# A K set between the first two Q sets, and two PSUM banks exchanged

## The chip, the cores and the metric

The kernel runs on one core of one Trainium2 chip. The metric is device time in microseconds. The engines are TensorE (PE in the profile, its weight loads apart as PEld), VectorE (DVE), ScalarE (ACT), GpSimd (POOL) and SyncE (SP), which issues most DMAs. Matrix products are written to PSUM, which this kernel divides into eight tiles of 128 x 512 fp32, called banks here.

## What is computed

Two branches read the same x (2048 rows of 512, bfloat16) and are mixed by a gate per row, g = sigmoid(sum(x * gate_w)):

- Branch B is an MLP: layer norm, product with w1 (512 x 1376), gelu, product with w2.
- Branch A is attention with a recurrent memory. The 2048 rows are cut into 64 segments of 32. Eight memory rows stand ahead of each segment, and attention runs over these 40 rows with 32 heads of 128:

```python
mem = mem0
for s in range(n_seg):                                  # 64, one after the other
    h = jnp.concatenate([mem, x[:, 32*s:32*s+32]], axis=1)      # 40 rows
    q, k, v = h @ Wq, h @ Wk, h @ Wv                    # 32 heads of 128
    p = softmax(where(mask, q @ k.T * scale, -1e9))
    o = (p @ v) @ Wo
    mem = o[:, :8]                                      # goes into the next segment
    outs.append(o[:, 8:])
out = g * concat(outs) + (1 - g) * mlp(x)
```

Segment s + 1 cannot project its memory rows before the attention of segment s has ended. The whole loop hangs on this recurrence.

## The kernel before

The program has three stages. First it does nearly all of the MLP (lines 299 to 598) while the attention weights are loaded; nine of its sixteen 128-row tiles are finished there, and for seven the second product is left over as filler. Then comes the loop over 64 segments (line 756), and last a short tail. The order of every instruction on every engine is written out by hand (a manual schedule); semaphores are added where one engine reads what another wrote, or overwrites what another still reads.

Four segments make a tile of 128 rows; T is the tile and si = 0..3 the segment's place in it. Of a segment's 40 rows, 32 are worked on in the loop itself: 24 rows of x and the 8 memory rows. They lie transposed in hT, which has four chunks (kc = 0..3) of 128 input features each. The other 8 rows of every segment, which are known ahead, are projected for a whole tile at once as filler work of the tile before.

One segment does, on TensorE in this order:

- Q and K of the 32 rows (lines 777 to 786). There are four groups: Q's first half of the heads, K's first half, Q's second half, K's second half. Group n is accumulated in bank U[n]. A group has four **sets**, one for each chunk kc of hT, and a set is four matmuls, one for each 32-column strip of the array (qk_unit, line 125). After each group ACT copies the bank to SBUF as bfloat16 (qk_cast, line 131) and DVE transposes the copy into QT or KT (qk_tr, line 136). After the first group DVE also writes the mask into U[0] (mask_put(1), line 257), where the second half of the scores is going to be.
- Scores of the first half (line 805), which read QT and KT, then the V sets in X1 and X2, sums of exponentials, scores of the second half.
- Attention times V (av, line 283), into all four U banks. ACT copies the result out: the memory's part into UT, the rest into XR.
- The output projection (wo_pass, line 736) into X2, which ACT copies to w in three pieces.
- The new memory (new_mem, line 744) in three calls, one for each piece of w. Call 0 makes chunk 0 of the next hT through bank U[0], call 1 chunk 1 through U[1], call 2 chunks 2 and 3 through a part of bank SbF. After each call DVE casts the product into hT (line 752). So the first Q set of the next segment needs the first cast, the second set the second, and the third and fourth sets the third.

Filler sets are spread between these steps by run(n). WS (line 755) says how many go where; one filler set goes between call 0 and call 1 and one between call 1 and call 2. A segment has eight filler sets. With si = 0 only five have gone by the first call, so that one set is left behind call 2; with other si none is left. In the last tile there is less filler.

In segments with si = 0, from the third tile on, extra (line 643) puts the finished rows of tile T - 2 together in a bank (out_sel, line 227) just before the first new_mem call. DVE reads that bank (line 238) after the third cast.

The lines that matter here, of the loop and of new_mem:

```python
for n, (t, hf) in enumerate(((0, 0), (1, 0), (0, 1), (1, 1))):
    bk = U[n]
    for kc in range(KC):
        qk_unit(bk, hc, t, hf, kc)
...
bk = (U[0][:, 0:M], U[1][:, 0:M], xs8z)[n]          # new_mem
```

Of the kernel before, what the change touches and what calls it, by code (L numbers as in the profile page):

```python
# [28 lines left out]
def kernel(ctx, tc, A_x, A_mem0, A_Wq, A_Wk, A_Wv, A_Wo, A_seg_len, B_x, B_w1, B_b1, B_w2, B_b2, gate_w, out):  # L29
# [4 lines left out]
    M = A_mem0.shape[1]  # L34
# [4 lines left out]
    KC = Dm // P  # L39
# [71 lines left out]
    U = [lps.tile([P, 512], FP32, name=f"U{i}") for i in range(4)]  # L111
# [13 lines left out]
    def qk_unit(bk, G, t, hf, kc):  # L125
        h0, h1 = HF[hf]
        for j in range(4):
            nc.tensor.matmul(bk[32 * j:32 * j + 32, :], lhsT=G[:, kc, :], rhs=W5[t][:, kc, h0:h1, j, :],  # L128
                             start=(kc == 0), stop=(kc == KC - 1), tile_position=(0, 32 * j))
# [57 lines left out]
    def vp_load(T, si):  # L187
        nc.sync.dma_start(VP[T % 2][:, si].rearrange("p v e -> p (v e)"), VLs[T][si:P:SPT].rearrange("p a v e -> p a (v e)"))
# [20 lines left out]
    def c_load(T):  # L209
        c = cw.tile([P, Dm], BF16, tag="c", name="c")  # L210
        nc.sync.dma_start(c[:], c_dr[T * P:(T + 1) * P, :])
        cs[T] = c
# [14 lines left out]
    def out_sel(T, bk):  # L227
        for si in range(SPT):
            nc.tensor.matmul(bk[32 * si:32 * si + 32, :], lhsT=SelR[:], rhs=ws.pop(SPT * T + si)[:], start=True, stop=False,
                             skip_group_check=True, tile_position=(0, 32 * si))  # L230
        wl = wls.pop(T)
        for si in range(SPT):
            nc.tensor.matmul(bk[32 * si:32 * si + 32, :], lhsT=SelL[:, 32 * si:32 * si + 32], rhs=wl[:], start=False, stop=True,
                             skip_group_check=True, tile_position=(0, 32 * si))

        def ev():
            o = cw.tile([P, Dm], BF16, tag="o", bufs=1, name="o")
            nc.vector.scalar_tensor_tensor(out=o[:], in0=bk[:], scalar=g_all[:, T:T + 1], in1=cs.pop(T)[:], op0=ALU.mult, op1=ALU.add)
            nc.sync.dma_start(out2[T * P:(T + 1) * P, :], o[:])
        dve_q.append(ev)  # L240
        yield

    def prep_h(s):
        T, si = divmod(s, SPT)
        nc.gpsimd.tensor_copy(out=hT[s % 3][:, :, 0:RIDE], in_=xTs[T][:, :, seg * si:seg * si + RIDE])
# [386 lines left out]
    def side(T, si):  # L632
        gens = []
        if si == 2:
            gens = [wo_left(T - 1, X1) if T >= 1 else mlp_units(8)]
        elif T + 1 == NT:
            gens = [mlp_units(4)] if si < 2 else []
        else:
            gens = [[left_qk(T + 1, 0, 0, X1), left_qk(T + 1, 1, 0, U[3])], [left_qk(T + 1, 0, 1, X1), left_qk(T + 1, 1, 1, U[3])], [],
                    [left_v(T + 1, 0, X1), left_v(T + 1, 1, U[3])]][si]  # L640
        return chain(*gens)

    def extra(T, si):

        if si == 0 and T >= 2:
            return out_sel(T - 2, U[2])
        return iter(())

    work = [(T, fc) for T in DEF for fc in range(FC)]
# [48 lines left out]
    xs8z = SbF[:, 4 * EW + NG:4 * EW + NG + 2 * M]  # L698
# [30 lines left out]
    def x_norm(s):  # L729
        T, si = divmod(s, SPT)  # L730
        XR, Rb = XRs.pop(s), Rbs.pop(s)[:].rearrange("p (c q) (h j) -> p h j c q", c=4, h=2)
        for out, o, a, b in ((UT[(s + 1) % 2], M, LEFT, 32), (UL[T % 2], LEFT * si, 0, LEFT)):
            for h in range(2):
                nc.gpsimd.tensor_tensor(out=out[:, :, 4 * h:4 * h + 4, o:o + b - a], in0=XR[:, :, 4 * h:4 * h + 4, a:b], in1=Rb[:, h, :, :, a:b], op=ALU.mult)  # L734
# [6 lines left out]
            nc.scalar.copy(out=w[:, a:b], in_=bk[:, a:b])  # L741
        return w

    def new_mem(w, hn, n):

        k0, nk = ((0, 1), (1, 1), (2, 2))[n]
        bk = (U[0][:, 0:M], U[1][:, 0:M], xs8z)[n]
        for k in range(nk):
            for c in range(4):
                nc.tensor.matmul(bk[32 * c:32 * c + 32, M * k:M * k + M], lhsT=w[:, (k0 + k) * P + 32 * c:(k0 + k) * P + 32 * c + 32], rhs=SelM[:],  # L750
                                 start=n < 2, stop=True, skip_group_check=True, tile_position=(0, 32 * c))
        nc.vector.tensor_copy(out=hn[:, k0:k0 + nk, RIDE:32], in_=bk.rearrange("p (k m) -> p k m", k=nk))  # L752


    WS = ((2, 2, 1), (2, 2, 2), (2, 2, 2), (2, 2, 2))
    for s in range(nseg):
        T, si = divmod(s, SPT)
        last = s == nseg - 1
        hc, hn = hT[s % 3], hT[(s + 1) % 3]
        W1, W2, W3 = WS[si]  # L760
        fill = side(T, si)
        if s + 1 < nseg:
            prep_h(s + 1)
        if s >= 1:
            x_norm(s - 1)
        if si == 0 and T >= 2:
            c_load(T - 2)
        if si < 3:
            vp_load(T, si + 1)
        if last:  # L770
            c_load(T - 1)
            c_load(T)
        if si == 0 and T + 2 < NT:
            load_xT(T + 2)
        if s in (2, (NT - 1) * SPT):
            hm_load4()
        for n, (t, hf) in enumerate(((0, 0), (1, 0), (0, 1), (1, 1))):
            bk = U[n]
            for kc in range(KC):
                qk_unit(bk, hc, t, hf, kc)  # L780
            if n == 0:
                flush(act_q, 9)
                flush(dve_q, 9)
            qk_tr(qk_cast(bk[:]), (QT, KT)[t], hf, LEFT * (1 - t))
            if n == 0:
                mask_put(1)
        V = cw.tile([P, NG, Dh], BF16, tag="V", name="V")
        E = cw.tile([P, NG, EW], BF16, tag="E", name="E")
        R = cw.tile([P, NG * 40], FP32, tag="R", name="R")
        Rs[s] = R  # L790
        xsum = SbF[:, 0:32 * NG].rearrange("p (i q) -> p i q", q=32)

        def exps(i2, x):
            c = slice(0, 40) if x else slice(40, EW)
            nc.scalar.activation(out=E[:, 4 * i2:4 * i2 + 4, c], in_=Sb[i2][:, :, c], func=ACTF.Exp, scale=scale)  # L795

        def msum(i2):
            sums(U[1 + 2 * i2][:, 320:352].rearrange("p (i q) -> p i q", q=8), E[:, 4 * i2:4 * i2 + 4, :], 40, 48, 8, True)

        def mnorm(i2):  # L800
            r, e = RP[i2], E[:, 4 * i2:4 * i2 + 4, 40:56].rearrange("p i (a q) -> p i a q", q=8)
            nc.vector.reciprocal(out=r, in_=U[1 + 2 * i2][:, 320:352])
            nc.vector.tensor_tensor(out=e, in0=e, in1=r.rearrange("p (i q) -> p i q", q=8).unsqueeze(2).to_broadcast([P, 4, 2, 8]), op=ALU.mult)

        scores(s, 0)
        nc.scalar.activation(out=E[:, 0:4, :], in_=Sb[0], func=ACTF.Exp, scale=scale)
        for kc in range(KC):
            v_unit(X1, hc, 0, kc)

        def v_cast(vb, h):  # L810
            i0 = 4 * vb + 2 * h
            nc.scalar.copy(out=V[:, i0:i0 + 2, :].rearrange("p i e -> p (i e)"), in_=(X1, X2)[vb][:, 256 * h:256 * h + 256])  # L812

        v_cast(0, 0)
        v_unit(X2, hc, 1, 0)
        if not last:
            xsums(E, 0)
            msum(0)
            mnorm(0)
        scores(s, 1)  # L820
        exps(1, 0)
        v_cast(0, 1)
        exps(1, 1)
        for kc in range(1, KC - 1):
            v_unit(X2, hc, 1, kc)
        if not last:
            if s:
                next(mlp, None)
            msum(1)
            mnorm(1)  # L830
        v_unit(X2, hc, 1, KC - 1)
        for h in range(2):
            v_cast(1, h)
        if last:
            break
        run(W1)
        if s:
            next(mlp, None)
        xsums(E, 1)
        recip_x(s)  # L840
        av(s, V, E)
        for j in (0, 2, 1, 3):
            nc.scalar.copy(out=UT[s % 2][:, j, :, 0:M], in_=U[j][:, 0:NG * 40].rearrange("p (i q) -> p i q", q=40)[:, :, 32:40])  # L843
        x_raw(s)
        run(W2)
        prep_q(s + 1)
        w = wo_pass(UT[s % 2], (0, P, 2 * P, Dm), X2)
        if s >= 1:
            ws[s - 1] = w
        run(W3)  # L850
        for _ in extra(T, si):
            pass
        new_mem(w, hn, 0)
        run(1)
        new_mem(w, hn, 1)
        run(1)
        new_mem(w, hn, 2)
        for _ in fill:
            pass
        if si == 3 and T + 2 < NT:  # L860
            left_x(T + 2)
        flush(dve_q, 9)
        nc.vector.tensor_tensor(out=rmin[:, 0:RW], in0=rmin[:, 0:RW], in1=R[:, 0:RW], op=ALU.min)
        flush(act_q, 9)
# [193 lines left out]
```

## Time and profile before

| | |
|---|---|
| median of 3 runs | 759.55 us (757.79 to 761.52) |
| profiled execution | 759.91 us, of which the span is 758.1 us |
| granted TensorE clock in it | 0.999 |
| TensorE busy | 741.6 us, 98% of the span |
| ACT, DVE, POOL busy | 71%, 53%, 36% |
| the loop over segments | from 80.4 us on; a segment takes about 10.2 to 10.5 us |

A row of the timeline gives the start in us from the start of the span, the duration, the engine, the line, the operation, output and inputs, shapes and the count of instructions that were merged into the row; in square brackets stands how long the engine was idle before it and what ended that. A row of the waits gives the engine and line that waited, what it waited for, the total in us, the number of times and the longest. Matmuls are pipelined: one of 512 columns has a duration of 0.38 us, but the next set starts long before it ends, so times between starts are what counts. The number before a bank or buffer is left out in the profile: U is any of U[0] to U[3].

### The profile page before, as it was taken

Reading aid. Unit: us, or ns where it says so; the run is one execution under the profiler, and the core shown is the slowest. Engines: PE = TensorE matmul, PEld = TensorE weight load, DVE = VectorE, ACT = ScalarE, POOL = GpSimd, SP = SyncE. Lnnn points to the kernel's source line nnn. Section 1 sums busy time; section 2 is a strip of 40 time slices with the busy share of each in tenths; the row PEclk is TensorE's granted clock in tenths of the full one; section 3 lists DMA queues with packets and bytes.
Section 4 is the critical chain, followed back from the end, with each engine's and each line's share of the span. In section 5 each row is a group of like instructions: output and inputs, shape, how many; then the busy total and the mean of one; then the engine's idle time right before and its main releaser. Section 6 shows DMA issues by size and latency. Waiting matters only on the chain.

```text
span 758.1 us, 45047 instructions
## 1 busy us (share of the span) xinstructions
PE 741.6 (98%) x19742; PEld 423.4 (56%) x19742; DVE 398.5 (53%) x1414; ACT 537.3 (71%) x1628; POOL 274.8 (36%) x517
## 2 busy tenths in 40 slices
PE   8999999999999999999999999999999999999997
PEld 5776455555555555555555556555555555555554
DVE  5767544545455545446454545445454545455454
ACT  5667677777777777777777777776777777677764
POOL 4001234433344343344333443434443344333441
PEclk9999999999999999999999999999999999999999
DMA  9999523222222323222222213231222212222222
GB/s 294 333 309 334 154 74 63 68 85 77 72 66 67 91 67 94 66 82 60 82 78 75 85 36 99 67 83 57 76 77 84 82 56 74 66 87 70 62 81 61
DMA packets 74971, 75.70 MB, mean 100 GB/s; under 512 B 42505, under 2 KB 64882, under 8 KB 73234
## 3 DMA queue, kind: packets, MB, share of 16 engines
q1 hardware_dynamic: 73730, 71.07, 30.7%
q8 instruction: 156, 2.56, 1.4%
q0 software_dynamic: 496, 1.18, 0.7%
q10 hardware_dynamic: 544, 0.52, 0.2%
q14 instruction: 45, 0.37, 0.2%
HBM read 59.49 MB, written 6.98 MB: 88 GB/s over the span
## 4 chain that ended last, share of the span: by engine, by line
PE 86%; issue 1%; ACT 0%; DVE 0%; DMA 0%; POOL 0%; DVEq 0%
PE U L128 33%; PE X L159 18%; PE X L147 17%; PE X L128 4%; PE U L290 3%; PE W L678 2%; PE U L147 2%; PE U L266 1%; PE U L750 1%; PE SbF L266 1%; PE SbF L705 1%; PE U L295 1%; PE U L277 1%; PE U L280 0%; PE U L270 0%
## 5 line engine op out<-in xcount | busy, mean ns | idle before, releaser
L734 POOL TENSOR_TENSOR UT<-XR,Rb 128x384 bf16<-128x384 bf16 x126 | 140.3, 1136 | 309.0 <-DMA Rb<-r_dr 237.8
L133 ACT CAST Tb<-U 128x512 bf16<-128x512 f32 x288 | 168.7, 586 | 81.8 <-PE U L128 78.9
L128 PEld LDWEIGHTS <-hT 128*32 128x32 bf16 x4096 | 107.6, 96 | 100.5 <-DVE hT L752 8.1
L147 PE MATMUL X<-Wv_sb,hT 128*32 128x512 bf16 x2048 | 144.6, 378 | 0.3 <-issue 0.2
L128 PE MATMUL U<-Wq_sb,hT 128*32 128x512 bf16 x2048 | 136.5, 381 | 0.2 <-DVE hT L752 0.2
L128 PE MATMUL U<-Wk_sb,hT 128*32 128x512 bf16 x2048 | 133.1, 379 | 0.0
L159 PE MATMUL X<-Wo_sb,UT 128*32 128x512 bf16 x2016 | 121.1, 380 | 0.0
L752 DVE CAST hT<-U 128x8 bf16<-128x8 f32 x126 | 20.9, 166 | 166.1 <-PE U L750 126.0
L812 ACT CAST V<-X 128x256 bf16<-128x256 f32 x256 | 88.7, 372 | 15.9 <-PE X L147 3.3
L137 DVE STREAM_TRANSPOSE QT<-Tb 128x256 f32<-128x256 f32 x128 | 56.6, 442 | 73.3 <-ACT Tb L133 72.5
L159 PEld LDWEIGHTS <-UT 128*32 128x32 bf16 x2048 | 56.4, 96 | 54.8 <-issue 14.3
L711 ACT CAST XR<-U 128x256 bf16<-128x256 f32 x252 | 78.5, 436 | 0.0
L741 ACT CAST w<-X 128x128 bf16<-128x128 f32 x189 | 44.8, 310 | 44.9 <-PE X L159 44.9
L137 DVE STREAM_TRANSPOSE KT<-Tb 128x256 f32<-128x256 f32 x128 | 57.0, 445 | 30.9 <-ACT Tb L133 23.2
L734 POOL TENSOR_TENSOR UL<-XR,Rb 128x128 bf16<-128x128 bf16 x126 | 60.3, 502 | 0.0
L147 PEld LDWEIGHTS <-hT 128*32 128x32 bf16 x2048 | 47.2, 94 | 21.6 <-issue 1.2
L726 POOL TENSOR_TENSOR racc<-racc,R 128x72 f32<-128x72 f32 x63 | 21.2, 336 | 93.6 <-DVE R L724 66.7
L843 ACT CAST UT<-U 128x64 bf16<-128x64 f32 x252 | 35.8, 226 | 26.4 <-PE U L295 26.2
L795 ACT ACTIVATE E<-U 128x64 bf16<-128x64 f32 (+1 forms) x128 | 35.0, 273 | 11.7 <-PE U L270 11.2
L480 PEld LDWEIGHTS <-w_sb 128*128 128x128 bf16 (+1 forms) x352 | 33.5, 100 | 15.1 <-issue 2.4
L750 PEld LDWEIGHTS <-w 128*32 128x32 bf16 x1008 | 23.6, 93 | 32.0 <-ACT w L741 25.2
L159 PE MATMUL X<-Wo_sb,UL 128*32 128x512 bf16 x512 | 39.4, 379 | 0.3 <-issue 0.3
(179 smaller groups left out, 1237.5 us busy)
## 6 DMA issues: line engine op xcount, KB each, us to landing
Rb<-r_dr SPq DMA_DIRECT2D x63, 512.0 KB, 4.0
Wv_sb<-in_A_Wv_dram SPq DMA_DIRECT2D x4, 1024.0 KB, 7.1
Wq_sb<-in_A_Wq_dram SPq DMA_DIRECT2D x4, 1024.0 KB, 8.7
Wk_sb<-in_A_Wk_dram SPq DMA_DIRECT2D x4, 1024.0 KB, 8.8
Wo_sb<-in_A_Wo_dram SPq DMA_DIRECT2D x4, 1024.0 KB, 11.3
VP<-VL SPq DMA_DIRECT2D x64, 64.0 KB, 3.5
hm<-h_dr SPq DMA_DIRECT2D x69, 32.0 KB, 2.1
c<-c_dr SPq DMA_DIRECT2D x16, 128.0 KB, 3.2
```

The costliest lines, as they stand in the source:

```text
L128: nc.tensor.matmul(bk[32 * j:32 * j + 32, :], lhsT=G[:, kc, :], rhs=W5[t][:, kc, h0:h1, j, :], start=(kc == 0), stop=(kc == KC - 1), tile_ ...
L133: nc.scalar.copy(out=Tb[:], in_=bk.rearrange("p (a b e) -> p a e b", a=8, b=2))
L137: nc.vector.transpose(out=dst[:, 8 * hf:8 * hf + 8, c0:c0 + 32, :].rearrange("p a r b -> p a (r b)").bitcast(FP32), in_=Tb[:].rearrange("p ...
L147: nc.tensor.matmul(bk[32 * j:32 * j + 32, :], lhsT=G[:, kc, :], rhs=Wv5[:, kc, 4 * vb:4 * vb + 4, j, :], start=(kc == 0), stop=(kc == KC - ...
L159: nc.tensor.matmul(bk[32 * c:32 * c + 32, :], lhsT=U_[:, j, i, :], rhs=Wo_sb[:, 4 * i + j, :], start=(n == 0), stop=(n == NW - 1), tile_po ...
L480: nc.tensor.matmul(hp[:rows, 0:TB * P], lhsT=w1_sb[:, kc, fc * P:fc * P + rows], rhs=yTs[blk][:, kc, :], start=(kc == 0), stop=(kc == KC - 1))
L711: nc.scalar.copy(out=XR[:, j], in_=U[j][:, 0:NG * 40].rearrange("p (i q) -> p i q", q=40)[:, :, 0:32])
L734: nc.gpsimd.tensor_tensor(out=out[:, :, 4 * h:4 * h + 4, o:o + b - a], in0=XR[:, :, 4 * h:4 * h + 4, a:b], in1=Rb[:, h, :, :, a:b], op=ALU ...
L741: nc.scalar.copy(out=w[:, a:b], in_=bk[:, a:b])
L795: nc.scalar.activation(out=E[:, 4 * i2:4 * i2 + 4, c], in_=Sb[i2][:, :, c], func=ACTF.Exp, scale=scale)
L812: nc.scalar.copy(out=V[:, i0:i0 + 2, :].rearrange("p i e -> p (i e)"), in_=(X1, X2)[vb][:, 256 * h:256 * h + 256])
L843: nc.scalar.copy(out=UT[s % 2][:, j, :, 0:M], in_=U[j][:, 0:NG * 40].rearrange("p (i q) -> p i q", q=40)[:, :, 32:40])
```

## The change

Three edits that belong together:

- In every segment the first set of the first K group (chunk 0) is issued right behind the first set of the first Q group, ahead of Q's second set. The K group's own loop then begins at chunk 1. Two groups are open at once, in two banks.
- The first K group is accumulated in U[2] instead of U[1], and the second Q group in U[1] instead of U[2].
- In segments with si = 0, out_sel puts its rows in U[1] instead of U[2], and the second new_mem call goes through U[2] instead of U[1]. In the other segments that call stays in U[1].

No instruction is added or removed.

```diff
     def extra(T, si):
         if si == 0 and T >= 2:
-            return out_sel(T - 2, U[2])
+            return out_sel(T - 2, U[1])
...
-    def new_mem(w, hn, n):
+    def new_mem(w, hn, n, si):
         k0, nk = ((0, 1), (1, 1), (2, 2))[n]
-        bk = (U[0][:, 0:M], U[1][:, 0:M], xs8z)[n]
+        bk = (U[0][:, 0:M], U[1 if si else 2][:, 0:M], xs8z)[n]
...
+    QK4 = ((0, 0), (1, 0), (0, 1), (1, 1))
...
-        for n, (t, hf) in enumerate(((0, 0), (1, 0), (0, 1), (1, 1))):
-            bk = U[n]
-            for kc in range(KC):
+        for n, (t, hf) in enumerate(QK4):
+            bk = U[(0, 2, 1, 3)[n]]
+            for kc in range(n == 1, KC):
                 qk_unit(bk, hc, t, hf, kc)
+                if n == kc == 0:
+                    qk_unit(U[2], hc, *QK4[1], 0)
...
-        new_mem(w, hn, 0)
+        new_mem(w, hn, 0, si)
```

The calls for the second and third product get the same new argument.

More of the change, by code (lines that the diff above doesn't have):

```diff
@@ L852 @@
             pass
-        new_mem(w, hn, 0)
+        new_mem(w, hn, 0, si)
         run(1)
-        new_mem(w, hn, 1)
+        new_mem(w, hn, 1, si)
         run(1)
-        new_mem(w, hn, 2)
+        new_mem(w, hn, 2, si)
         for _ in fill:
```

## The prediction

> **What bounds the kernel now.** I read the page first: its busy shares, clock row and chain.
>
> ```profile
> span 758.1 us, 45047 instructions
> PE 741.6 (98%) x19742; PEld 423.4 (56%) x19742; DVE 398.5 (53%) x1414; ACT 537.3 (71%) x1628; POOL 274.8 (36%) x517
> ...
> PEclk9999999999999999999999999999999999999999
> ...
> q8 instruction: 156, 2.56, 1.4%
> ...
> PE 86%; issue 1%; ACT 0%; DVE 0%; DMA 0%; POOL 0%; DVEq 0%
> ```
>
> TensorE holds 86% of the chain and no other engine as much as 1%. Its clock is full all along. So only what TensorE itself loses counts, and work on other engines costs nothing until TensorE has to wait for it. Next the list of waits, for TensorE (PE) and its weight loads (PEld).
>
> ```profile
> PEld L750 <- ACT w L741: 25.2, 65, 0.9
> PEld L159 <- issue: 16.3, 49, 1.3
> PEld L705 <- ACT E L806: 14.0, 60, 0.2
> PEld L128 <- DVE hT L752: 8.1, 47, 0.4
> ...
> PE U L295 <- issue: 2.5, 4, 1.1
> ...
> PE X L147 <- issue: 1.3, 3, 0.9
> ```
>
> The fourth row is where the change acts: 47 times the weight load of a Q or K set (L128) waits for the cast that puts new memory columns into hT (L752), 8.1 us in all, 0.17 us each. That is idle time of the weight loads. They normally run ahead of the matmuls, so what TensorE loses must be read from the starts of the matmuls, in the timeline.
>
> Segment 32, the start of a tile (si = 0):
>
> ```profile
> 413.10 0.43 DVE L752 CAST hT<-U 128x8 bf16<-128x8 f32 x2 [2.44 <-PE U L750]
> ...
> 413.33 1.11 PE L128 MATMUL U<-Wq_sb,hT 128*32 128x512 bf16 x16
> ...
> 413.58 2.95 PEld L128 LDWEIGHTS <-hT 128*32 128x32 bf16 x60 [0.16 <-DVE hT L752]
> 413.60 0.17 DVE L752 CAST hT<-SbF 128x16 bf16<-128x16 f32 x1
> ...
> 414.27 1.04 PE L128 MATMUL U<-Wk_sb,hT 128*32 128x512 bf16 x16
> 414.49 0.58 ACT L133 CAST Tb<-U 128x512 bf16<-128x512 f32 x1 [0.34 <-PE U L128]
> ...
> 415.11 0.45 DVE L137 STREAM_TRANSPOSE QT<-Tb 128x256 f32<-128x256 f32 x1 [1.20 <-ACT Tb L133]
> 415.13 1.04 PE L128 MATMUL U<-Wq_sb,hT 128*32 128x512 bf16 x16
> 415.36 0.58 ACT L133 CAST Tb<-U 128x512 bf16<-128x512 f32 x1 [0.28 <-PE U L128]
> ...
> 415.48 0.37 DVE L259 CAST U<-MkF 128x224 f32<-128x224 bf16 x1
> 415.97 0.45 DVE L137 STREAM_TRANSPOSE KT<-Tb 128x256 f32<-128x256 f32 x1
> ...
> 415.99 1.04 PE L128 MATMUL U<-Wk_sb,hT 128*32 128x512 bf16 x16
> ...
> 416.86 0.27 PE L266 MATMUL SbF<-QT,KT 128*32 128x40 bf16 x16
> ```
>
> A group is 16 matmuls, four sets of four. From the first K group to the last one are two groups: 415.99 - 414.27 = 1.72 us, so an undisturbed group takes 0.86 and a set 0.215. The first Q group takes 414.27 - 413.33 = 0.94. Its first set goes at once; the second needs the second cast, done at 413.10 + 0.43 = 413.53, and its weights load at 413.58, 0.05 later, where an undisturbed second set would already run at 413.55. The third needs the cast that ends at 413.77. So one set of 0.215 us is all the cover, and it is too short. Other tiles show whether this is the rule:
>
> ```profile
> 101.85 1.11 PE L128 MATMUL U<-Wq_sb,hT 128*32 128x512 bf16 x16
> 102.78 1.04 PE L128 MATMUL U<-Wk_sb,hT 128*32 128x512 bf16 x16
> ...
> 740.52 1.11 PE L128 MATMUL U<-Wq_sb,hT 128*32 128x512 bf16 x16
> 741.45 1.04 PE L128 MATMUL U<-Wk_sb,hT 128*32 128x512 bf16 x16
> ```
>
> ```profile
> 382.19 0.41 DVE L752 CAST hT<-U 128x8 bf16<-128x8 f32 x2 [2.57 <-ACT w L741]
> 382.41 3.34 PEld L128 LDWEIGHTS <-hT 128*32 128x32 bf16 x64
> 382.60 1.05 PE L128 MATMUL U<-Wq_sb,hT 128*32 128x512 bf16 x16
> 382.74 0.75 DVE L238 SCALAR_TENSOR_TENSOR o<-U,g_all,c 128x512 bf16<-128x512 f32 x1
> 383.46 1.05 PE L128 MATMUL U<-Wk_sb,hT 128*32 128x512 bf16 x16
> ...
> 384.33 1.05 PE L128 MATMUL U<-Wq_sb,hT 128*32 128x512 bf16 x16
> ```
>
> At both ends of the loop the first Q group takes 0.93. At 382.60, a segment with si = 1, it takes 0.86: there, by the order of the code, one filler set stands between the last new-memory product and the first Q set, and the weights of all 64 matmuls load without a wait. That row is an experiment made by the kernel itself: one more set of cover takes the whole wait away.
>
> **The change, part by part.** *One K set moved up.* In every segment the first K set goes between the first and second Q sets. It reads the same weights (hT, chunk 0) as the set before it and needs no further cast. No instruction is added on any engine, and no DMA, so no queue changes. In segment 32 Q's second set is then due at 413.33 + 2 x 0.215 = 413.76, 0.18 after its weights could load; the third at 413.98, against a cast that ends at 413.77 and may be used at 413.82. Both waits are covered. The saving is 0.94 - 0.86 = 0.08 there and 0.93 - 0.86 = 0.07 at the ends, 0.07 to 0.08 a segment. Times 47 waits that is 3.3 to 3.8 us; some of the 47 are shorter, so I take 3.4.
>
> The other end of this term: were the whole idle time of the row TensorE's, the saving would be 8.1 us; were it all covered, nothing. The starts of the matmuls stand between and are nearest to the case itself, so 3.4 stays. The Trainium skill (TensorE: Matmul & The Clock Gate, section The mechanism) says that a weight load overlaps running matmuls only when they use another row group. All four column tiles here use all rows, so by that rule no load would run ahead, the idle time would be TensorE's in full, and the sum would be 8.1 us. This trace disagrees: the 2.95 us of loads at 413.58 lie beside matmuls that start every 0.215.
>
> *What comes later.* The first Q group now ends one set later relative to its start, so its cast starts at 413.33 + 4 x 0.215 + 0.44 = 414.63 instead of 414.49 (0.44 is the distance now: 414.49 less the start of that group's last set, 414.27 - 0.215). It ends at 415.21. The K group ends 0.08 earlier than now, and its cast starts at 415.28: ACT is free, by 0.07. On DVE the order is QT transpose, mask (L259), KT transpose: QT at 415.25 to 415.70, mask to 415.99 with the overlap that the rows show (it starts 0.08 before the transpose ends) or 416.07 without, KT to 416.44 or 416.52, against 416.42 now. The scores, which read KT, come at 416.86 - 0.08 = 416.78. With 0.05 for the signal 0.21 to 0.29 us stay. Cost nothing, with DVE's slack as the cover; without it each 0.1 us would cost 6.3 us over 63 segments. The casts of the later groups keep their distance to TensorE.
>
> *Banks.* K's first group takes U2 and Q's second U1. In a segment with si other than 0 the second new-memory product stays in U1, so K's first set waits for no cast. With si = 0 the output rows (out_sel) move to U1 and that product to U2, so in the next segment K's first set waits for its cast: at 382.19 + 0.41 + 0.05 = 382.65, while the set is due at 382.60 + 0.215 = 382.82. Cost nothing; cover 0.17 us. All of TensorE's queue stands behind that matmul, so whatever is lacking there is lost in full: were the cast 0.05 later than the cover allows, 0.05 us in each of some 16 segments, 0.8 us. The read of the output rows (L238) ends at 383.49, and U1 is not needed before 384.33, just as U2 is now.
>
> *Sum.* The profiled execution took 759.91 us, 1.81 over its span; 759.91 - 3.4 = 756.5. It lies 0.36 above the median of the runs, 759.55, so the median should come to 756.2, 0.45% less. Runs of this kernel lie between 757.79 and 761.52, so I treat 0.5%, 3.8 us, as what can be told from no change; the forecast stands almost on that line.
>
> **Rivals.** *The gain is eaten by instruction supply.* The issue rows show TensorE and its loads waiting for nothing that the profile has, up to 1.3 us at once. If such a stall ends when a transfer of instructions lands, and that transfer was under way before the Q group, a faster Q group only makes the stall longer. Were all 49 segments of the L159 row like this, 49 x 0.07 = 3.4 would be gone and the time 759.5. Against it: 16.3 us over 49 is 0.33 each, and the long ones can only be few. The Trainium skill (Runtime: NRT & Kernel Launch, section Instruction fetch mechanics) says that instructions come in blocks of 16 KiB through a DMA queue of the engine's own; the q8 row, 2.56 MB in 156 packets, agrees in size. By that rule this rival is possible, and it would give 759.5.
>
> *More is gained.* If the altered timing spares the 2.5 and 1.3 us of direct issue stalls (L295, L147), 3.8 in all, the time would be 752.4; with half of it 754.3. [...] Against it: no instruction is removed, and nothing in the new order makes them shorter.
>
> *Slower: KT comes late.* Place: DVE between the first Q cast and the scores. One segment already shows it:
>
> ```profile
> 469.43 0.42 DVE L137 STREAM_TRANSPOSE KT<-Tb 128x256 f32<-128x256 f32 x1
> ...
> 469.90 0.17 PEld L266 LDWEIGHTS <-KT 128*32 128x32 bf16 x16 [0.39 <-DVE KT L137]
> ```
>
> There KT ended at 469.85 and the scores' weights came 0.05 later, behind an idle time of 0.39. It decides once KT ends more than 0.21 us later than worked out above. At 0.35 us later the scores would lose 0.14 in 63 segments, 8.8 us: 756.2 + 8.8 = 765.0. Speaks for it: the QT transpose and the mask do move later by a set, and the mask stands between them and KT. Against it: the margin is over twice the shift that the sum gives KT.
>
> *The change does nothing*, since a third wait stands right behind: the only later cast of hT is the one that ends at 413.77, and it is covered, so I count this with the first rival.
>
> **How the numbers follow.** Forecast (stall gone, gain kept) 0.66, between 754.3 and 758.1 by the spread of the runs, 1.9 to each side. Gain eaten 0.10, at 759.5. More gained 0.14, between 752.4 and 754.3. KT late 0.10, at 765. The line of 0.5% is at 759.55 x 0.995 = 755.75, close enough to 756.2 that I split the forecast evenly. Faster: 0.33 + 0.14 = 0.47. Same: 0.33 + 0.10 = 0.43. Slower: 0.10. The range 753.0 to 760.2 takes in the forecast, the eaten gain with some noise, and about half of the larger gain: 0.83.
>
> **What would show it.** Right: the wait of L128's loads for L752 falls from 47 times and 8.1 us to next to nothing; the first Q set and first K set start 0.215 apart; from the first Q set to the scores 3.45 us where segment 32 has 3.53; the casts and KT at the distances given. Wrong, in this order of likelihood: issue rows that grow by what the Q group saves, a new row in which L266's loads wait for KT in most segments, or a wait of K's first set in U2.

## The result, and the profile after

The changed kernel takes 757.5 us (median of 20 runs, 755.42 to 760.59) where the kernel before takes 760.03 (median of 20, 757.79 to 761.81). The ratio is 0.9967, with a 95% interval of 0.9954 to 0.9981: faster by 2.5 us, and by less than the 0.5% that the prediction drew as its line. Measured again in two later groups of runs, each beside its own runs of before, the ratio was 0.9951 (0.9932 to 0.9971) and 0.9989 (0.9965 to 1.0013).

The page of the profiled execution gives the span, and the chain by engine:

```profile
span 754.9 us, 45034 instructions
...
PE 86%; DVE 1%; issue 1%; ACT 0%; DMA 0%; POOL 0%; DVEq 0%
```

The list of waits (what waited, for what, us in total, times, longest):

```profile
PEld L159 <- issue: 15.4, 49, 0.5
PEld L705 <- ACT E L809: 14.4, 62, 0.2
...
PEld L750 <- ACT w L741: 25.1, 65, 0.9
...
PEld L128 <- DVE hT L752: 0.6, 2, 0.3
```

The page counts 13 instructions fewer than before, although none was removed: ten of them are matmul records that the trace lacks, since the weight loads are 19742 in both. TensorE is the bound as before, and of the 47 waits of L128's loads for the casts, 8.1 us, two with 0.6 us are left. The waits around it have hardly moved: 25.1 and 14.4 us, against 25.2 and 14.0. The timeline shows the same place as in the prediction, segment 32, engine by engine:

```profile
414.35 0.43 DVE L752 CAST hT<-U 128x8 bf16<-128x8 f32 x2 [2.44 <-PE U L750]
414.85 0.17 DVE L752 CAST hT<-SbF 128x16 bf16<-128x16 f32 x1
...
414.57 3.14 PEld L128 LDWEIGHTS <-hT 128*32 128x32 bf16 x64
...
415.89 1.29 ACT L133 CAST Tb<-U 128x512 bf16<-128x512 f32 x2 [0.47 <-PE U L128]
...
414.59 0.39 PE L128 MATMUL U<-Wq_sb,hT 128*32 128x512 bf16 x4
414.80 0.39 PE L128 MATMUL U<-Wk_sb,hT 128*32 128x512 bf16 x4
415.02 0.82 PE L128 MATMUL U<-Wq_sb,hT 128*32 128x512 bf16 x12
415.67 0.82 PE L128 MATMUL U<-Wk_sb,hT 128*32 128x512 bf16 x12
...
418.04 0.27 PE L266 MATMUL SbF<-QT,KT 128*32 128x40 bf16 x16
...
416.51 0.45 DVE L137 STREAM_TRANSPOSE QT<-Tb 128x256 f32<-128x256 f32 x1 [1.34 <-ACT Tb L133]
416.88 0.37 DVE L259 CAST U<-MkF 128x224 f32<-128x224 bf16 x1
417.21 0.45 DVE L137 STREAM_TRANSPOSE KT<-Tb 128x256 f32<-128x256 f32 x1
```

All 64 loads are one row now, with no wait in it. Q's first set, K's first set and Q's second start at 414.59, 414.80 and 415.02, 0.215 apart. From the first Q set to the scores it is 418.04 - 414.59 = 3.45 us, where it was 416.86 - 413.33 = 3.53. The second cast ends at 414.78 and the third at 415.02, 0.24 and 0.21 us ahead of the sets that need them (415.02 and 415.23). Counted from the first Q set, QT and mask start 0.14 us later than before on DVE (1.92 and 2.29 us, where they were 1.78 and 2.15). KT does not: it starts 0.03 behind the end of ACT's K cast (417.18), as before, and ends 3.07 us after the first Q set where it was 3.09. That is at 417.66, 0.38 ahead of the scores.

The shortest segment of each place in the tile, over the third to the fifteenth tile, shows the gain with the least noise: between the starts of the first Q sets it was 10.53, 10.16, 10.23 and 10.23 us for si = 0 to 3, and is 10.455, 10.157, 10.152 and 10.153. The place with the filler set behind the last product (si = 1) stayed, and the three others are 0.07 to 0.08 shorter.

### The profile page after: what moved, and what is told of

It reads as the page before. It is cut to its first block, busy times and chain, and to the rows that moved or that the text cites. A ratio compares the mean times of both kernels' runs of the same rounds, so it can differ in the third digit from the quotient of the medians.

```text
span 754.9 us, 45034 instructions
## 1 busy us (share of the span) xinstructions
PE 737.8 (98%) x19732; PEld 423.0 (56%) x19742; DVE 400.1 (53%) x1414; ACT 537.7 (71%) x1628; POOL 275.2 (36%) x517
## 4 chain that ended last, share of the span: by engine, by line
PE 86%; DVE 1%; issue 1%; ACT 0%; DMA 0%; POOL 0%; DVEq 0%
PE U L128 32%; PE X L159 19%; PE X L147 16%; PE X L128 4%; PE U L290 3%; PE W L678 2%; PE U L147 2%; PE U L266 1%; PE U L750 1%; PE SbF L266 1%; PE SbF L705 1%; PE U L295 1%; DVE E L806 1%; PE U L277 1%; PE U L280 0%
## 5 line engine op out<-in xcount | busy, mean ns | idle before, releaser
L128 PEld LDWEIGHTS <-hT 128*32 128x32 bf16 x4096 | 107.8, 96 | 97.2 <-DVE hT L752 0.6
L147 PE MATMUL X<-Wv_sb,hT 128*32 128x512 bf16 x2048 | 144.6, 378 | 0.4 <-issue 0.4
L128 PE MATMUL U<-Wq_sb,hT 128*32 128x512 bf16 x2048 | 144.2, 379 | 0.4 <-DVE hT L752 0.4
L128 PE MATMUL U<-Wk_sb,hT 128*32 128x512 bf16 x2048 | 144.2, 379 | 0.0
L147 PEld LDWEIGHTS <-hT 128*32 128x32 bf16 x2048 | 47.1, 94 | 21.8 <-issue 1.3
L750 PEld LDWEIGHTS <-w 128*32 128x32 bf16 x1008 | 23.6, 93 | 31.9 <-ACT w L741 25.1
L128 PE MATMUL X<-Wq_sb,GL 128*32 128x512 bf16 x496 | 38.6, 381 | 1.4 <-issue 1.3
## 6 DMA issues: line engine op xcount, KB each, us to landing
Wo_sb<-in_A_Wo_dram SPq DMA_DIRECT2D x4, 1024.0 KB, 11.3
```

## The experiments

All times are beside runs of the kernel before on the same chip. They are medians; gains and losses in us are taken from the ratio over all runs, which can differ from that of the two medians by up to 0.15%. "Lost in the first Q group" is worked out from the starts of the matmuls in the trace: summed over all 64 segments, the time from the start of the first set to that of the sixth, less five times 0.2157 us, the undisturbed distance of two sets. For the kernel before it is 3.40 us, for the changed one 0. The diffs are against the changed kernel.

### Order alone

```diff
-            return out_sel(T - 2, U[1])
+            return out_sel(T - 2, U[2])
...
-        bk = (U[0][:, 0:M], U[1 if si else 2][:, 0:M], xs8z)[n]
+        bk = (U[0][:, 0:M], U[1][:, 0:M], xs8z)[n]
...
-            bk = U[(0, 2, 1, 3)[n]]
+            bk = U[n]
...
-                    qk_unit(U[2], hc, *QK4[1], 0)
+                    qk_unit(U[1], hc, *QK4[1], 0)
```

> K's first set moved up, but all banks as in the kernel before (K in U1, output rows in U2, second new-memory product always in U1). My theory: the saving is the cover of one more set ahead of the second and third casts. Here K's first set must itself wait until the second cast has read U1: done and signalled at 413.58 in segment 32 of before, the set due at 413.55, so about 0.04 us is lost at this place in the 46 segments or so that lost 0.07, and half of the gain is left: 1.7 us faster than before. The load wait of L128 for L752 goes, and a matmul wait of L128 for L752 of about 0.04 us x 46 = 1.7 us comes. Rival (the banks alone bring the gain): no gain, 0 us. Rival (order alone is enough, banks do not matter): the whole 2.5 to 3.4 us.

Measured: 757.62 against 759.62 us, ratio 0.9978 (0.9962 to 0.9995), 1.7 us faster. The waits and the timeline at segment 34 (one with si = 2):

```profile
PEld L128 <- issue: 9.6, 50, 1.2
```

```profile
434.64 0.44 DVE L752 CAST hT<-U 128x8 bf16<-128x8 f32 x2 [2.52 <-PE U L750]
...
434.88 0.39 PE L128 MATMUL U<-Wq_sb,hT 128*32 128x512 bf16 x4
435.13 0.40 PE L128 MATMUL U<-Wk_sb,hT 128*32 128x512 bf16 x4
435.35 0.83 PE L128 MATMUL U<-Wq_sb,hT 128*32 128x512 bf16 x12
...
435.13 2.92 PEld L128 LDWEIGHTS <-hT 128*32 128x32 bf16 x59 [0.16 <-issue]
```

The second cast ends at 435.08 and K's first set starts 0.05 later, 0.25 after Q's first instead of 0.215, and nothing is lost behind it; 1.58 us are lost in the first Q groups of all segments, about half of 3.40. The wait is not listed under the name that was expected. I read the row of issue waits as what it held up, the loads of the other 59 matmuls: 0.16 us here and 50 times in all, where the kernel before has this row 4 times. The order alone brings about half of the gain, and the banks the other half on top of it.

### Banks alone

```diff
-            for kc in range(n == 1, KC):
+            for kc in range(KC):
                 qk_unit(bk, hc, t, hf, kc)
-                if n == kc == 0:
-                    qk_unit(U[2], hc, *QK4[1], 0)
```

> All bank edits of the change, but the K sets in their old order. My theory: the same time as before within its noise (0 us, at most 0.3 us either way), and the wait of L128's loads for L752 again about 47 times and 8 us. Rival (the exchange of banks brings the gain, by freeing a bank earlier): 2.5 us faster than before.

Measured: 760.38 against 759.62 us, ratio 1.0025 (1.0002 to 1.0048). The wait is back, to the number:

```profile
PEld L128 <- DVE hT L752: 8.2, 47, 0.4
```

3.33 us are lost in the first Q groups. The banks bring nothing by themselves. The interval lies just above 1, a loss of 0.2 to 3.6 us where 0.3 at most was expected. No row of this trace shows where it would be, but the profiled execution, 753.01 us, is the fastest of the twelve.

### The output rows left in U2

```diff
-            return out_sel(T - 2, U[1])
+            return out_sel(T - 2, U[2])
...
-        bk = (U[0][:, 0:M], U[1 if si else 2][:, 0:M], xs8z)[n]
+        bk = (U[0][:, 0:M], U[1][:, 0:M], xs8z)[n]
```

> The changed order with K's first group in U2 and Q's second in U1, but the output rows stay in U2 and the second new-memory product always goes through U1. My theory: in the segments with si = 1 from the third tile on, 14 of them, K's first set now waits until DVE has read the output rows out of U2: that ended at 383.49 in before, signalled at 383.54, and the set is due at 382.82, so 0.72 us x 14 = 10 us is lost, and the time is about 757.5 + 10 = 767.6, slower than before by 7.5 us. All other segments keep the gain. Rival (the moved rows are only tidiness, the wait is hidden): as the changed kernel, 757.5.

Measured: 764.51 against 759.62 us, ratio 1.0079 (1.0054 to 1.0104): slower than before by 6.0 us. The waits, and the timeline of segment 33 (si = 1):

```profile
PE U L128 <- DVE o L238: 7.8, 14, 0.7
```

```profile
425.62 0.40 PE L128 MATMUL U<-Wq_sb,hT 128*32 128x512 bf16 x4
426.56 0.40 PE L128 MATMUL U<-Wk_sb,hT 128*32 128x512 bf16 x4 [0.55 <-DVE o L238]
...
425.76 0.75 DVE L238 SCALAR_TENSOR_TENSOR o<-U,g_all,c 128x512 bf16<-128x512 f32 x1
```

The read of the output rows ends at 426.51, and K's first set starts 0.05 later, 0.94 after Q's first in place of 0.215: 0.72 us, in 14 segments. The list counts only the 0.55 that the engine stood empty. 14 x 0.72 = 10 us less the gain of 3.4 in the other segments is 6.7, and 6.0 was measured. This is the third edit of the change seen from the other side: without it the moved set costs more than it gains.

### One, two and three sets moved up

```diff
-            for kc in range(n == 1, KC):
+            for kc in range(2 * (n == 1), KC):
                 qk_unit(bk, hc, t, hf, kc)
-                if n == kc == 0:
-                    qk_unit(U[2], hc, *QK4[1], 0)
+                if n == 0 and kc < 2:
+                    qk_unit(U[2], hc, *QK4[1], kc)
```

> Two sets of the first K group go up: Q0 K0 Q1 K1 Q2 Q3 K2 K3. The wait is already covered by one, so the second brings nothing; it only makes Q's first group end another set (0.215 us) later. In the profile of the changed kernel (segment 32, first Q set at 414.59) the QT transpose starts 1.92 us after the first Q set, the mask 2.29, the KT transpose ends at 3.07, and the scores start at 3.45. Here QT starts at 2.14, the mask at 2.50, KT at 2.83 and ends at 3.28; with 0.05 for the signal 3.33, still 0.12 ahead of the scores. My theory: the same time as the changed kernel, within its noise. Rival (KT late, the margin is already used up): scores wait, slower than the changed kernel by 0.1 us or more a segment, 6 us.

Measured: 757.35 against 759.25 us, ratio 0.9974 (0.996 to 0.9988), as the changed kernel. With 3 in place of both 2s:

> Three sets up: Q0 K0 Q1 K1 Q2 K2 Q3 K3. QT at 2.35 us after the first Q set, mask at 2.72, KT ends at 3.50, signalled at 3.55; the scores are due at 3.45. My theory: now the margin is gone, and the scores' weight loads wait for the KT transpose in nearly every segment, 0.10 us x 63 = 6 us: slower than the changed kernel by 4 to 9 us, and a row in the waits, L266's loads for KT's L137, of more than 50 times. Rival (DVE's chain has more room than worked out, or the scores are bound by something else): no slower than the changed kernel.

Measured: 759.35 against 759.25 us, ratio 1.0007 (0.9994 to 1.002): in these runs the whole gain is gone. The timeline of two up, segment 34, and of three up, segment 34, with the row of its waits:

```profile
434.90 0.39 PE L128 MATMUL U<-Wq_sb,hT 128*32 128x512 bf16 x4
...
438.35 0.27 PE L266 MATMUL SbF<-QT,KT 128*32 128x40 bf16 x16
...
437.68 0.42 DVE L137 STREAM_TRANSPOSE KT<-Tb 128x256 f32<-128x256 f32 x1
```

```profile
435.97 0.39 PE L128 MATMUL U<-Wq_sb,hT 128*32 128x512 bf16 x4
...
439.44 0.28 PE L266 MATMUL SbF<-QT,KT 128*32 128x40 bf16 x16
...
439.44 0.17 PEld L266 LDWEIGHTS <-KT 128*32 128x32 bf16 x16 [0.34 <-DVE KT L137]
...
438.69 0.37 DVE L259 CAST U<-MkF 128x224 f32<-128x224 bf16 x1
438.97 0.42 DVE L137 STREAM_TRANSPOSE KT<-Tb 128x256 f32<-128x256 f32 x1
```

```profile
PEld L266 <- DVE KT L137: 21.8, 64, 0.4
```

With one set up KT ends 3.07 us after the first Q set (3.01 in segment 34), with two 3.20, with three 3.42, and the scores start at 3.45, 3.45 and 3.47. So the margin is used up by three, the loads then wait in every segment, and the rival of the late KT is real, two sets further on than the change goes. The loss was mis-sized: 0.02 us at the scores, not 0.10, because KT ends at 3.42 and not at 3.50. I had taken 0.33 from the start of the mask to KT, and 0.45 for KT, from segment 32 of the changed kernel. There KT starts right behind ACT's K cast, and that sets the 0.33; here it starts 0.28 after the mask, 0.09 before the mask's end, and takes 0.42. The list gives 21.8 us for a wait that moves the scores by 0.02 us a segment. The shortest segments grow by 0.03 (10.19 for 10.155), 63 x 0.03 = 1.9 us. The ratio is 0.4% above that of the changed kernel, 3 us, so the 4 to 9 us expected were too many. The other 1.1 us lie within the intervals, and no row of the loop shows them; the last section names a place behind the loop where this profile loses 2 us more than that of the changed kernel.

### K's first set behind Q's second

```diff
-                if n == kc == 0:
+                if n == 0 and kc == 1:
                     qk_unit(U[2], hc, *QK4[1], 0)
```

> The changed kernel with K's first set behind Q's second set in place of Q's first: Q0 Q1 K0 Q2 Q3. It tells the two waits apart. The second cast is then covered by one set as in before (0.035 to 0.04 us lost, by the 413.53 + 0.05 against 413.55 of segment 32), the third cast by three, and nothing is lost on it. My theory: half of the gain, 46 x 0.037 = 1.7 us slower than the changed kernel, 1.7 us faster than before; the row of L128's loads waiting for L752 stays at some 46 times, with less time each. Rival (the third cast is what cost): the whole gain. Rival (the second cast alone cost, the third was only pushed): no gain lost at the third, so the same 1.7.

Measured: 757.82 against 759.25 us by medians, but the ratio is 0.9996 (0.9976 to 1.0017), which cannot tell no gain from one of 1.7 us. The trace tells more:

```profile
PEld L128 <- DVE hT L752: 8.2, 47, 0.4
```

```profile
436.21 0.65 PE L128 MATMUL U<-Wq_sb,hT 128*32 128x512 bf16 x8
436.69 0.39 PE L128 MATMUL U<-Wk_sb,hT 128*32 128x512 bf16 x4
...
436.46 2.93 PEld L128 LDWEIGHTS <-hT 128*32 128x32 bf16 x60 [0.16 <-DVE hT L752]
```

The loads wait as often and as long as before (I had expected less time each). TensorE loses 0.04 at the second set and another 0.01 at the next, which waits for no later cast: 436.69 - 436.21 = 0.48 for two sets of 0.215. I read the 0.01 as loads that start late and need a set to get ahead again. Over all segments 2.27 us are lost. So of 3.40 the third cast's part was 1.1, and the second cast's 2.3, more than the half I had put there. The trace of before agrees: there the second, third and fourth set of such a segment come 0.039, 0.024 and 0.010 us late, and 46 x 0.024 is 1.1. The list of waits cannot tell this kernel from the one before; the starts of the matmuls can.

### Two attempts at a faster version

The longest regular wait left is that of the first new-memory product for w, 25.1 us in the list. The second half-set of the MLP was moved there from its place ahead of the sums of exponentials:

```diff
         run(W1)
-        if s:
-            next(mlp, None)
...
+        if s:
+            next(mlp, None)
         new_mem(w, hn, 0, si)
```

> An attempt at a faster version. The regular wait that is left in the changed kernel is that of the first new-memory product for w (matmuls 0.31 us apart where 0.2 is usual, in segments without output rows). The second filler half-set of the MLP (0.1 us) is taken from its place ahead of the sums of exponentials and put right ahead of that product. My theory: the place it is taken from stands ahead of waits for ACT and DVE too (attention times V needs the last V cast and the normalised E), so most of the gain comes back there: within 1.5 us of the changed kernel. Rival (that place has slack): 0.1 us x 46 = 4 to 5 us faster than the changed kernel.

Measured: 760.01 against 759.25 us, ratio 1.0013 (0.9995 to 1.003), 0.46% above the 0.9967 of the changed kernel, 3.5 us. Its waits, and its timeline over the two places, then that of the changed kernel:

```profile
PEld L750 <- ACT w L741: 12.0, 51, 0.6
```

```profile
440.94 0.22 PE L705 MATMUL SbF<-BO,E 128*32 128x4 bf16 x8
...
442.09 1.91 PE L159 MATMUL X<-Wo_sb,UT 128*32 128x512 bf16 x32
...
444.37 0.19 PE L750 MATMUL U<-SelM,w 128*32 128x8 bf16 x4
```

```profile
441.89 0.22 PE L705 MATMUL SbF<-BO,E 128*32 128x4 bf16 x8
...
442.93 1.91 PE L159 MATMUL X<-Wo_sb,UT 128*32 128x512 bf16 x32
...
445.20 0.19 PE L750 MATMUL U<-SelM,w 128*32 128x8 bf16 x4
```

The wait in the list was halved, and the time rose. From the output projection to the product it is 2.28 us with the filler and 2.27 without: here, in segment 34, ACT's copies set it, whatever TensorE does meanwhile. From the sums to the projection it rose from 1.04 to 1.15, so the filler was worth its 0.1 us where it stood. In the segments with si = 0 the product did not wait, since the output rows are put together ahead of it; there the filler lengthens the way from the projection to the product too, from 2.37 to 2.48. Their shortest segment grows by 0.12 us, the others by 0.03 to 0.04. Over all segments that is 3.4 us, against 3.5 measured.

The second attempt is about a row of the changed kernel's first segment, where GpSimd's QT is late. First the changed kernel, then the one before:

```profile
85.45 0.28 PE L266 MATMUL SbF<-QT,KT 128*32 128x40 bf16 x16 [2.20 <-POOL QT L249]
```

```profile
84.74 0.28 PE L266 MATMUL SbF<-QT,KT 128*32 128x40 bf16 x16 [0.68 <-POOL QT L249]
```

```diff
+    prep_q(0)
     for i in range(2):
         nc.gpsimd.memset(UT[i][:, :, :, M:32], 0.0)
-    prep_q(0)
```

> The changed kernel with one edit at a place that its profile showed: in the first segment the scores waited 2.20 us for GpSimd's QT (L249), which stood behind two memsets of UT (1.42 us together) that nothing needs so early. Here that copy goes ahead of the memsets. Both wait for the same DMAs, so QT should be ready 1.4 us sooner, and the scores of the first segment start 0.7 to 1.4 us sooner (TensorE would arrive there 0.7 us ahead of QT in the profile of before, 2.2 us in that of the changed kernel). My theory: 1 us faster than the changed kernel, which is a third of the spread of single runs, and a POOL wait in that row of under 1 us. Rival (QT then waits longer for its DMAs, or the time is lost later): the same as the changed kernel.

Measured: 756.68 us, ratio to before 0.9979 (0.9958 to 1.0001), beside the changed kernel in the same group:

> The changed kernel beside the one above, on the same chip: a third measurement of the change. My theory, from 3.4 us taken off TensorE in every run: a ratio to before of 0.9955 within the interval, as in the two before it (0.9967 and 0.9951). Rival (about a quarter of it is always eaten later): the interval lies above 0.9955.

Measured: 757.14 us, ratio 0.9989 (0.9965 to 1.0013). The profile of the new version:

```profile
82.02 0.42 POOL L249 COPY QT<-QL 128x128 f32<-128x128 f32 x1 [12.43 <-DMA VP<-VL]
82.38 1.43 POOL L616 MEMSET UT<- 128x768 bf16 x2
...
83.17 0.28 PE L266 MATMUL SbF<-QT,KT 128*32 128x40 bf16 x16
```

QT now lands at 82.44, and the scores start at 83.17 with no wait for it, 3.49 us after the first Q set (79.68). In the profile of the changed kernel beside it they start at 84.01, 4.25 us after the first Q set (79.76): 0.76 us saved. That is shown by the trace; the runs, 0.46 us apart with intervals of 0.2% to either side, cannot confirm it.

### The change measured again

> The changed kernel once more, on the chip of the three others and beside the same runs of before. My theory: the steady part of the loop gains 0.07 us in some 47 segments, 3.4 us, and what is measured differs from that by instruction stalls that fall differently in every run: a ratio of 0.9955 to 0.998. Rival (a fixed part of the gain, about 0.9 us, is eaten by longer instruction stalls in every run): the summed excess of the segments over their undisturbed length grows against before by about 0.9 us in this profile too.

Measured: 755.29 against 759.62 us, ratio 0.9951 (0.9932 to 0.9971).

## Why the prediction was right, point by point

- **The stall and its cover.** Right, in place, size and number: 45 of the 47 waits are gone; 46 segments lost time in the trace of before, 45 of them 0.07 us, 3.40 us in all, and after the change the sum is 0. Order alone left half of it, banks alone left all of it, and moving the set one place further left two thirds (2.27 of 3.40), so it is the cover ahead of the casts that counts.
- **3.4 rather than 8.1 us.** Right. Loads waited 8.1 us and TensorE lost 3.4; the kernel with K behind Q's second set has the same 8.2 us in the list and loses 2.27. The row-group rule of the Trainium skill (TensorE: Matmul & The Clock Gate, section The mechanism), by which the loads could not run ahead, does not hold for these column tiles: after the change the 64 loads run beside the matmuls in one row without a wait. The same section also lets a load run ahead into a background weight buffer, which the prediction left out; that would fit these rows, and no run here tests it.
- **What comes later.** Right that it costs nothing. KT ends 3.07 us after the first Q set, where 3.11 to 3.19 was worked out: the sum put KT behind the mask, and it comes right behind ACT's K cast. The margin, tried by moving more sets, holds for two and is used up by three.
- **The banks.** Right: in the segments with si = 1 the second cast in U2 cost nothing (10.157 us a segment, as before; in segment 9 alone K's first set comes 0.04 us late), and the exchange of the output rows is what keeps 0.72 us x 14 away.
- **The sum.** 756.2 was forecast and 757.5 measured: 2.5 us gained where 3.4 was the term. The three measurements give 2.5, 3.7 and 0.8 us. The first two intervals hold 0.9955, which is 3.4 us; the third, from 0.9965 on, does not. So by the first two nothing needs to be missing, and by the third at least 0.8 us is. An estimate from all three, weighted by their intervals, is 0.9967 with 0.9957 to 0.9977, or 1.8 to 3.3 us: a little less than 3.4. Of the 1.3 us between 756.2 and 757.5 the base is 0.5: the forecast started from a median of 759.55 over 3 runs, and over 20 it is 760.03. The range of 753.0 to 760.2 holds the old time too, so the time alone would not have shown the prediction right; the traces and the interval do.
- **The rival of more gained.** Not seen. In this profile the issue waits of L295 and L147 fell from 2.5 and 1.3 us to 1.1 and 1.0, but that of another line (L128, into an X bank) rose from 0.3 to 1.3.
- **The rival of the eaten gain.** Not settled. From the first Q set of segment 1 to that of segment 63 the profiles take 648.8 us before and 645.1, 644.5 and 642.2 in three profiles of the changed kernel. Against the shortest segment of each kind, the changed kernel's three are 11.0, 10.4 and 8.1 us too long. The kernel before is too long by 11.3 by its own shortest segments, and the one with the banks alone by about 6. The excess after lies inside the scatter of the old order, so it did not visibly grow, but one profile each cannot show 0.9 us. That the stalls are instruction supply was never tested. What I left at a chance of 0.10 as all or nothing may hold in part.

## What to carry to other kernels

Where an engine alternates with another over a short chain, what counts is the number of independent instructions between producer and user; a set that needs only the first piece of the data, taken from a later group, cost nothing here and covered the pieces that follow. Before it is moved, ask of its output bank who reads it last: here two of the three edits exist only for that, and without one of them the same move costs 6 us. A total in the list of waits is a bound and not a price: the same 8 us cost 3.4 in one kernel and 2.3 in another, 21.8 us cost 2 in a third, and halving a row of 25 us made a fourth one slower, so price a wait by the starts of the matmuls.

## What was not expected

Single profiles of one order differ by more than the change is worth. The old order shows spans of 758.1 and, with the banks alone exchanged, 751.2 us, although both lose 3.3 to 3.4 us at the casts. Part of it is the loop's excess (11.3 and about 6 us), in which single segments are up to 1.4 us longer. Some of them are the same ones again and again: 3, 12, 21, 24, 27, 37, 42 and 48 were longer than usual by 0.2 us or more in both profiles of the old order and in all three of the changed kernel. Others differ from profile to profile. So the place in the program has a part in these stalls, and their length differs from run to run; what they wait for is not shown. Part of the spread is the first segment: GpSimd waited for the VP DMAs, QT was ready at 84.7, 85.4 and 84.0 us in three profiles, and the scores lost 0.68, 2.20 and 0.62 us there.

Six profiles also lose time behind the loop, where no experiment meant to change anything. TensorE's last branch (L944 in the changed kernel, past a fallback that is not needed) is the row to look at, first in the changed kernel, then with three sets up:

```profile
L944 PEldq COMPARE_BRANCH  x1: 1249/1249/1249, 751.9 to 751.9; - x1
```

```profile
L944 PEldq COMPARE_BRANCH  x1: 3939/3939/3939, 753.1 to 753.1; - x1
```

It takes 1.2 to 1.8 us before, in the three profiles of the changed kernel, with the banks alone and with QT first. It takes 3.0 to 3.9 us with the order alone, the rows in U2, two and three sets up, K behind Q's second set and the late filler, and from the first Q set of the last segment to the end of the span it is 18.9 to 19.6 us in these and 17.3 to 17.6 in the others. Why, and whether every run of these six has it, is not shown. So their times can hold up to 2 us that have nothing to do with the loop, and the starts of the matmuls, which lie ahead of it, are the safer measure.
